# Layer norm by Ln and Exp under one activation table, eight token tiles transposed as pairs of 64 rows, and a new order of blocks 0 to 11 in an attention kernel

## The chip, the cores and the metric

The kernel runs on one core of a Trainium2 chip. The metric is the device time in microseconds of one execution; three runs of the kernel before gave 785.58, 786.32 and 788.21 us, median 786.32.

The core's engines work side by side, each through its own queue in order: TensorE (PE) multiplies matrices, VectorE (DVE), ScalarE (ACT) and GpSimd (POOL) work on elements, and SyncE (SP) issues most of the DMAs. A matmul writes to PSUM, from where DVE or ACT copies its result to SBUF. Engines wait for each other through semaphores only.

## The reference

The core of what is computed, with S = 2048 tokens, D = 640, 32 heads of 192, and a window of 512 keys per head:

```python
xn = _layernorm(x, axis=-1)                       # (x - m) / sqrt(v + 1e-5)
q = (xn @ wq).reshape(B, Sq, Hq, Dh)
k, v = k_cache[:, :, Sk - W:, :], v_cache[:, :, Sk - W:, :]
p = _softmax(einsum("bhqd,bhkd->bhqk", q, k) * (Dh ** -0.5), axis=-1)
s = einsum("bhqk,bhkd->bhqd", p, v).reshape(B, Sq, Hq * Dh) @ wo
...
r = xn @ w_r                                      # the two best tokens by r
idx = argsort(-r)[:, :2]
y = (silu(x_sel @ w_gate) * (x_sel @ w_up)) @ w_down * sigmoid(r_sel)
g = silu(xn + scatter of y to the rows idx)
return x + s * g
```

The output is 1 x 2048 x 640 in bf16. The change lies in the layer norm, in the transposes behind it, and in the order of the first part of the attention.

## The kernel before

Tokens are 16 tiles of 128 rows; four tiles make a token group (t5 = 0 to 3). Heads go in groups of four, two pairs each. A *step* is a head group, a token group and a head pair; it has two *blocks*, and a block covers two tiles (a = 0, 1) of one head pair. There are 128 blocks.

A block b goes through these items:

- **S.b.a** (scores, line 350): six matmuls of 64 rows into one of two PSUM tiles of two banks each (pool ps_s). A third S therefore waits until the exponentials of the one two before it are done.
- **M.b.a** (row_max, line 362): the negated row maximum on DVE.
- **E.b.a** (exps, line 382): two exponentials on ACT, then a DMA transpose of the result on SP's queue (for each a by itself where the item ends in .s or split is set, else one for both after a = 1).
- **P.b** (o_item, line 457): 32 matmuls with v; DVE or ACT scales the output (lines 449 and 452, letters v and a), and a DMA transpose follows. It stands two blocks behind S.
- **W.k** (w_item, line 504): 24 matmuls with wo; the sums go to s_acc.

Ahead of a step stand its queries: **q.i.c** (q_whole, line 294) makes one of three columns with 128-row matmuls; **qa** and **qb** (q_phase, line 315) make one or two columns with 64-row matmuls in two phases, the second of which waits for a later row maximum. All but S share four PSUM banks (pool ps_f) during the first 12 blocks; a new tile waits until the bank that it gets has been read.

**The head.** Blocks 0 to 11 are written out by hand in the list FIRST (line 651), read token by token by first (line 571); every engine gets its instructions in the order of that list. In it also stands all of the layer norm, group by group as x arrives:

- lx, lk, lq, x, k, v, wq, wo (and gk, gq, gv, gw for head group 1) issue loads on SP or ACT; x.2 loads token group 2 into the buffer that group 0 has used.
- bn and st are statistics of half a tile on DVE (bn_stats, with bn_aggr after the second half); **sa.t5.q.c** (rows, line 543) does the same for tile q on ACT, by a sum (c = 0) and a sum of squares (c = 1), with tiny GpSimd steps behind it.
- dev is a square root on ACT for one tile of group 0, app a reciprocal and the normalisation on DVE.
- nw.t5.j is one of seven steps for the deviation of a whole group (rsqrt_parts, line 218: Ln, Exp, an addition on GpSimd, three DVE steps of one Newton round; then nmr = -mean x rstd).
- **ap.n** normalises tile n on GpSimd, ACT or DVE (letters g, a, v), **turn.n** transposes it: five 128 x 128 transposes on PE into one bank, and one copy to xnT.
- ko, kT, kturn, gT: K reordered on GpSimd and transposed; wd copies half of a wo piece to the other 64 partitions on GpSimd (line 150, 1.78 us each), which W reads.
- exp loads the activation table that has both Ln and Exp. Ahead of it, the square root of line 253 uses another table.

From block 12 on a loop (line 1001) goes through BLOCK, the same items in a fixed order:

```python
BLOCK = "A S0 M0 W m E0 B S1 M1 P E1 l".split()
```

The expert's input (m_gather, line 803) has its own layer norm on 2 rows around block 40.

Of the kernel before, what the change touches and what calls it, by code (L numbers as in the profile page):

```python
# [21 lines left out]
def kernel(ctx, tc, A_x, A_k_cache, A_v_cache, A_wq, A_wo, B_x, B_w_r, B_w_gate, B_w_up, B_w_down, out):  # L22
# [158 lines left out]

    def ln_apply(eng, n, src):
        if eng == "a":
            nc.scalar.activation(out=xn[:, n, :], in_=src, func=ACT.Identity, bias=nmr[:, n:n + 1], scale=rstd[:, n:n + 1])
            return
        (nc.gpsimd if eng == "g" else nc.vector).tensor_scalar(
            out=xn[:, n, :], in0=src, scalar1=rstd[:, n:n + 1], scalar2=nmr[:, n:n + 1], op0=ALU.mult, op1=ALU.add)
# [30 lines left out]
    def rsqrt_parts(var_ap, out_ap):  # L218

        T = {}  # L220

        def ln():
            T["v"] = small.tile([P, 4], FP32, name="nw_v")
            T["a"] = small.tile([P, 4], FP32, name="nw_a")
            nc.scalar.activation(out=T["a"], in_=var_ap, func=ACT.Ln, bias=eps_t[:, 0:1], scale=1.0)

        def ex():
            nc.scalar.activation(out=out_ap, in_=T["a"], func=ACT.Exp, scale=-0.5)
# [43 lines left out]
    def turn_tile(n, copy):  # L272
        tp = f_tile([P, DC, P], BF16, "tp")
        for dc in range(DC):
            nc.tensor.transpose(out=tp[:, dc, :], in_=xn[:, n, dc * P:(dc + 1) * P], identity=ident)  # L275
        copy(out=xnT[:, n], in_=tp)  # L276

# [811 lines left out]
```

## Time and profile before

| what | value |
|---|---|
| median of three runs | 786.32 us |
| the profiled execution, whole / span of its trace | 785.81 / 784.0 us |
| PE busy | 771.7 us (98%) |
| DVE, ACT, POOL busy | 561.2, 566.2, 327.1 us |
| granted TensorE clock, mean | 0.999 |
| S.0.0 starts / S.12.0, the first of the loop, starts | 10.53 / 85.39 us |

A profile row by line and tile reads: line, engine, operation, output <- input, shapes, count | busy us, mean ns of one | idle of its engine ahead of it and what ended most of it. A row in order of time reads: start in us, length in us, engine, line, operation, tiles, count, and in brackets the idle time ahead of it with what released it. A row of a stage reads: its bounds and length, then busy time (and instructions) of PE, PE's weight loads, DVE, ACT and POOL, the granted clock, the DMA share and GB/s. In the chain of waits a row is a piece of the chain that ended last: start, length, engine, tile and line.

### The profile page before, as it was taken

Reading aid. Unit: us, or ns where it says so; the run is one execution under the profiler, and the core shown is the slowest. Engines: PE = TensorE matmul, PEld = TensorE weight load, DVE = VectorE, ACT = ScalarE, POOL = GpSimd, SP = SyncE. Lnnn points to the kernel's source line nnn. Section 1 sums busy time; section 2 is a strip of 40 time slices with the busy share of each in tenths; the row PEclk is TensorE's granted clock in tenths of the full one; section 3 lists DMA queues with packets and bytes.
Section 4 is the critical chain, followed back from the end, with each engine's and each line's share of the span. In section 5 each row is a group of like instructions: output and inputs, shape, how many; then the busy total and the mean of one; then the engine's idle time right before and its main releaser. Section 6 shows DMA issues by size and latency. Waiting matters only on the chain.

```text
span 784.0 us, 27247 instructions
## 1 busy us (share of the span) xinstructions
PE 771.7 (98%) x11384; PEld 572.0 (73%) x11384; DVE 561.2 (72%) x952; ACT 566.2 (72%) x1420; POOL 327.1 (42%) x281
## 2 busy tenths in 40 slices
...
GB/s 233 201 173 171 173 177 184 147 193 161 169 213 177 180 200 203 185 178 189 204 187 195 187 188 200 173 189 173 179 172 174 150 189 165 187 181 158 196 197 104
DMA packets 447132, 142.19 MB, mean 181 GB/s; under 512 B 414180, under 2 KB 446438, under 8 KB 447008
## 3 DMA queue, kind: packets, MB, share of 16 engines
...
q0 software_dynamic: 1024, 2.85, 1.3%
...
## 4 chain that ended last, share of the span: by engine, by line
PE 93%; DVE 4%; ACT 2%; DMA 0%; issue 0%; DVEq 0%; ACTq 0%
PE w L482 26%; PE q_ps L332 24%; PE o_ps L435 21%; PE s L359 20%; DVE nm L364 1%; PE q_ps L301 1%; ACT pexp L386 1%; DMA x_in<-in_A_x_dram 0%; DVE stats L538 0%; DVE o_sb L449 0%; ACT xnT L276 0%; DVE qT L305 0%; PE gu_ps L836 0%; PE tp L275 0%; DVE stats L248 0%
## 5 line engine op out<-in xcount | busy, mean ns | idle before, releaser
L364 DVE TENSOR_REDUCE nm<-s 128x2 f32<-128x1024 f32 x256 | 313.0, 1223 | 153.3 <-PE s L359 151.2
L386 ACT ACTIVATE pexp<-s,nm 128x512 bf16<-128x512 f32 x508 | 342.6, 688 | 94.7 <-DVE nm L364 91.0
L332 PE MATMUL q_ps<-xnT,wq_g 64*128 64x512 bf16 (+1 forms) x2340 | 232.7, 323 | 0.0
L482 PE MATMUL w<-wo_g,oT 64*128 64x320 bf16 x3072 | 231.4, 296 | 0.0
L359 PE MATMUL s<-kT,qT 64*128 64x512 bf16 x1536 | 211.6, 376 | 1.7 <-ACT pexp L386 1.4
L482 PEld LDWEIGHTS <-oT 64*128 64x128 bf16 x3072 | 172.0, 94 | 55.7 <-DMA oT<-o_sb 0.5
L435 PEld LDWEIGHTS <-pT 64*128 64x128 bf16 x4096 | 176.3, 94 | 30.6 <-issue 2.8
L435 PE MATMUL o_ps<-v_sb,pT 64*128 64x192 bf16 (+1 forms) x4096 | 193.7, 243 | 2.8 <-DMA pT<-pexp 1.6
L452 ACT ACTIVATE o_sb<-o_ps,rl 128x192 bf16<-128x192 f32 x250 | 91.6, 418 | 97.3 <-PE o_ps L435 88.3
L332 PEld LDWEIGHTS <-wq_g 64*128 64x128 bf16 x2340 | 125.1, 100 | 46.5 <-DVE qT L305 0.5
L150 POOL COPY wo_g<-wo_g 64x1920 bf16<-64x1920 bf16 x32 | 56.9, 1781 | 195.4 <-DMA wo_g<-in_A_wo_dram 180.2
L359 PEld LDWEIGHTS <-qT 64*128 64x128 bf16 x1536 | 84.9, 94 | 56.5 <-issue 2.4
L515 DVE TENSOR_TENSOR s_acc<-s_acc,w 128x320 f32<-128x320 f32 x192 | 84.9, 484 | 30.7 <-PE w L482 30.7
L386 ACT ACTIVATION_READ_ACCUMULATOR pexp<-s,nm 128x1 f32 x460 | 94.0, 204 | 0.0
L344 ACT ACTIVATE qT<-q_ps 128x1024 bf16<-128x1024 f32 x114 | 92.2, 809 | 0.1
L449 DVE TENSOR_TENSOR o_sb<-o_ps,rl 128x384 bf16<-128x384 f32 x131 | 73.0, 557 | 12.1 <-PE o_ps L435 2.2
L926 POOL TENSOR_SCALAR yh<-y_bc,oh 128x640 f32<-128x640 f32 x32 | 60.4, 1886 | 5.7 <-DMA y_bc<-y_d 2.9
L120 POOL COPY k_perm<-k_raw 128x768 bf16<-128x768 bf16 x30 | 24.3, 827 | 89.0 <-DMA k_raw<-in_A_k_cache_dram 64.3
L927 POOL TENSOR_TENSOR xn<-xn,yh 128x640 bf16<-128x640 bf16 x32 | 45.0, 1406 | 2.7
L913 POOL TENSOR_SCALAR tz<-tz 128x640 f32<-128x640 f32 x16 | 11.7, 728 | 63.7 <-ACT tz L912 63.7
L986 POOL TENSOR_TENSOR s_acc<-s_acc,x_fin 128x640 f32<-128x640 f32 x16 | 22.4, 1400 | 11.8 <-DMA x_fin<-in_A_x_dram 10.9
L914 POOL TENSOR_TENSOR xn<-tz,xn 128x640 bf16<-128x640 f32 x16 | 22.4, 1400 | 1.3
...
## 6 DMA issues: line engine op xcount, KB each, us to landing
...
```

What stands on the lines that cost most here:

```text
L150: nc.gpsimd.tensor_copy(out=grp[g][("wo", pr)][half(1), cs, :], in_=grp[g][("wo", pr)][half(0), cs, :])
L332: mm = nc.tensor.matmul(q_ps[k][:, 0:n] if type(q_ps) is list else q_ps[:, k, 0:n], lhsT=wq[half(r), dc, c:2 * Dh:3], rhs=xnT[half(r), tok ...
L344: nc.scalar.activation(out=out, in_=q_ps[:, :, 0:n], func=ACT.Copy, scale=scale)
L359: nc.tensor.matmul(s_of[b, a][:, r, :], lhsT=qT_of[i][half(r), c, u * P:(u + 1) * P], rhs=grp[g][("kT", pr)][half(r), :, c, :], start=(c = ...
L364: rm = nc.vector.tensor_reduce(out=nm_of[b, a], in_=s_of[b, a], axis=AX.X, op=ALU.max, negate=True)
L386: nc.scalar.activation(out=p_of(b, a)[:, :, hh, :].rearrange("p (x j) e -> p x j e", x=2), in_=s_of[b, a][:, hh, :].rearrange("p (j e x) - ...
L435: nc.tensor.matmul(o_of[b][r][:, a, 0:n], lhsT=pT_ring[half(r), b % RP, a, k, :], rhs=v_ring[half(r), (g * PAIRS + pr) % RV, k, 0:n], star ...
L449: nc.vector.tensor_tensor(out=o_sb, in0=src, in1=rl[:, r].unsqueeze(2).unsqueeze(3).to_broadcast([P, 2, 3, HK]), op=ALU.mult)
L452: nc.scalar.activation(out=o_sb[:, a], in_=src[:, a], func=ACT.Copy, scale=rl[:, r, a:a + 1])
L482: nc.tensor.matmul(w_ps[r][:, 0:cs.stop - cs.start], lhsT=oT_ring[half(r), bs[pr] % RT, c, :], rhs=grp[g][("wo", pr)][half(r), c, cs], sta ...
L515: nc.vector.tensor_tensor(out=acc, in0=acc, in1=src, op=ALU.add)
L926: nc.gpsimd.tensor_scalar(out=yh, in0=M["y_bc"][:, j, :], scalar1=M["oh"][:, n, j:j + 1], scalar2=None, op0=ALU.mult)
```

## The change

- **The deviation.** For all groups, rstd is Exp(-0.5 Ln(var + eps)) on ACT (ln_rstd); the Newton round, the addition on GpSimd and group 0's square root and reciprocal are gone. nw has two steps now: ln_rstd, and nmr. The token exp, which loads the table with Ln and Exp, stands ahead of all ACT work; before it stood behind M.0.0.
- **The normalisation.** DVE takes (x - mean) x rstd, GpSimd x rstd + nmr; ACT takes none. The expert's norm takes (x - mean) x rstd too.
- **The pairs.** Tiles 4 to 11 are turned two at a time (token tt, turn_pair): 20 transposes of 64 rows against a 64 x 64 identity, the upper 64 rows of both tiles into one bank and the lower ones into another, and two copies of 640 elements per partition.
- **q_phase** can take two tiles of a step (ha, hb; not used in the new list) and copy its result on either engine. Step 3 has its columns 0 and 1 by qa and qb now.
- **The order.** FIRST is new throughout. Statistics on ACT: tiles 8, 9, 11, 12, 14 (before 12, 13, 14), so ten passes for six. x.2 is read first by sa.2.0.0, which stands behind q.1.2 and ahead of S.1.0. wq.1 is loaded ahead of k.1.0; wd.1 to wd.3 stand in blocks 3 to 5 with sa passes ahead of them on GpSimd's queue. E.4.0, E.8.0 and E.9.0 send their transposes by halves.

```diff
+    def ln_rstd(out, var):
+        t = small.tile([P, 4], FP32, name="ln_v")[:, 0:out.shape[-1]]
+        nc.scalar.activation(out=t, in_=var, func=ACT.Ln, bias=eps_t[:, 0:1], scale=1.0)
+        nc.scalar.activation(out=out, in_=t, func=ACT.Exp, scale=-0.5)
+
+
+    def ln_nmr(bs):
+        nc.vector.scalar_tensor_tensor(out=nmr[:, bs], in0=mv[:, bs, 0], scalar=-1.0, in1=rstd[:, bs], op0=ALU.mult, op1=ALU.mult)
+
     def ln_apply(eng, n, src):
-        if eng == "a":
-            nc.scalar.activation(out=xn[:, n, :], in_=src, func=ACT.Identity, bias=nmr[:, n:n + 1], scale=rstd[:, n:n + 1])
-            return
-        (nc.gpsimd if eng == "g" else nc.vector).tensor_scalar(
-            out=xn[:, n, :], in0=src, scalar1=rstd[:, n:n + 1], scalar2=nmr[:, n:n + 1], op0=ALU.mult, op1=ALU.add)
-
-    def ln_nmr(mean_ap, rstd_ap, nmr_ap):
-        nc.vector.scalar_tensor_tensor(out=nmr_ap, in0=mean_ap, scalar=-1.0, in1=rstd_ap, op0=ALU.mult, op1=ALU.mult)
+        if eng == "g":
+            nc.gpsimd.tensor_scalar(out=xn[:, n, :], in0=src, scalar1=rstd[:, n:n + 1], scalar2=nmr[:, n:n + 1], op0=ALU.mult, op1=ALU.add)
+        else:
+            nc.vector.tensor_scalar(out=xn[:, n, :], in0=src, scalar1=mv[:, n, 0:1], scalar2=rstd[:, n:n + 1], op0=ALU.subtract, op1=ALU.mult)
...
-    def rsqrt_parts(var_ap, out_ap):
-
-        T = {}
-
-        def ln():
-            T["v"] = small.tile([P, 4], FP32, name="nw_v")
-            T["a"] = small.tile([P, 4], FP32, name="nw_a")
-            nc.scalar.activation(out=T["a"], in_=var_ap, func=ACT.Ln, bias=eps_t[:, 0:1], scale=1.0)
-
-        def ex():
-            nc.scalar.activation(out=out_ap, in_=T["a"], func=ACT.Exp, scale=-0.5)
-
-        def v():
-            nc.gpsimd.tensor_scalar(out=T["v"], in0=var_ap, scalar1=EPS, scalar2=None, op0=ALU.add)
-
-        def s1():
-            nc.vector.scalar_tensor_tensor(out=T["a"], in0=out_ap, scalar=-0.5, in1=out_ap, op0=ALU.mult, op1=ALU.mult)
-
-        def s2():
-            nc.vector.tensor_tensor(out=T["a"], in0=T["a"], in1=T["v"], op=ALU.mult)
-
-        def s3():
-            nc.vector.scalar_tensor_tensor(out=out_ap, in0=T["a"], scalar=1.5, in1=out_ap, op0=ALU.add, op1=ALU.mult)
-        return [ln, ex, v, s1, s2, s3]
...
+    def first_apply(n):
+        ln_apply("v", n, x_in[0][:, n, :])
+
     def first_dev(n):
-        nc.scalar.activation(out=rstd[:, n:n + 1], in_=mv[:, n, 1:2], func=ACT.Sqrt, bias=eps_t[:, 0:1], scale=1.0)
-
-    def first_apply(n):
-        nc.vector.reciprocal(out=rstd[:, n:n + 1], in_=rstd[:, n:n + 1])
-        nc.vector.tensor_scalar(out=xn[:, n, :], in0=x_in[0][:, n, :], scalar1=mv[:, n, 0:1], scalar2=rstd[:, n:n + 1],
-                                op0=ALU.subtract, op1=ALU.mult)
+        ln_rstd(rstd[:, n:n + 1], mv[:, n, 1:2])
...
+    def turn_pair(n, es):
+        tp = [f_tile([P, 2, DC, P // 2], BF16, "tp") for _ in range(2)]
+        for u in range(2):
+            for dc in range(DC):
+                for r in range(2):
+                    nc.tensor.transpose(out=tp[r][:, u, dc, :], in_=xn[half(r), n + u, dc * P:(dc + 1) * P], identity=ident[half(r), half(r)])
+        for r in range(2):
+            copies[es[r]](out=xnT[:, n:n + 2, :, half(r)], in_=tp[r])
...
-        return ([bn(q, c) for q in range(4) for c in range(nsub)], rsqrt_parts(mv[:, bs, 1], rstd[:, bs]) + [lambda: ln_nmr(mv[:, bs, 0], rstd[:, bs], nmr[:, bs])],
+        return ([bn(q, c) for q in range(4) for c in range(nsub)], [lambda: ln_rstd(rstd[:, bs], mv[:, bs, 1]), lambda: ln_nmr(bs)],
...
+        elif op == "tt":
+            turn_pair(n[0], e)
...
-    lx.0.s lx.1.a lk.0.s lk.1.s lq.0.a lx.2.s lx.3.s v.0 x.1.0 bn.0.0 bn.1.0 x.1.1 bn.1.1 dev.1 bn.0.1 app.1 dev.0 k.1.0 app.0 bn.2.0 turn.0.a bn.3.0 bn.3.1 turn.1.a v.1 kturn.av bn.2.1 wq.1 dev.3 q.0.2.0.a k.1.1 q.0.0.0.v dev.2 v.2 q.0.1.0.a
-    ko.1 app.2 app.3 st.1.0
-    S.0.0 M.0.0 exp x.2 turn.2.a turn.3.a S.0.1 kT.1 M.0.1 st.1.1 E.0.0.s st.1.2 wo.0 q.0.1.1.a q.0.0.1.a q.0.2.1.v E.0.1
-    S.1.0 wo.1 st.1.3 st.1.4 S.1.1 M.1.0 st.1.5 E.1.0.s q.1.1.a M.1.1 q.1.2.a E.1.1 st.1.6 q.1.0.v st.1.7 nw.1.0
-    S.2.0 nw.1.1 nw.1.2 M.2.0 wo.2 S.2.1 nw.1.3 nw.1.4 nw.1.5 M.2.1 nw.1.6 st.2.0 E.2.0.s ap.7.g ap.6.v P.0.vv E.2.1
-    S.3.0 M.3.0 ap.4.a v.3 S.3.1 turn.6.a ap.5.g wd.0 turn.5.a turn.4.v turn.7.v E.3.0.s st.2.1 st.2.2 P.1.va M.3.1 wo.3 st.2.3 E.3.1 q.2.1.a q.2.2.v st.2.4 wd.1 q.2.0.v P.2.va
-    S.4.0 M.4.0 S.4.1 E.4.0 x.3 M.4.1 st.2.5 q.3.1.a E.4.1 wd.2 st.2.6 st.2.7 nw.2.0 q.3.2.a nw.2.1 nw.2.2
-    S.5.0 M.5.0 nw.2.3 E.5.0 nw.2.4 q.3.0.v S.5.1 wd.3 nw.2.5 sa.3.0.0 nw.2.6 M.5.1 E.5.1 sa.3.2.0 W.0.v ap.10.g
-    S.6.0 ap.11.g M.6.0 gk.0 E.6.0 ap.9.g ap.8.v W.1.v P.3.av S.6.1 M.6.1 P.4.va
-    S.7.0 st.3.6 E.6.1 turn.10.v turn.11.v turn.9.a turn.8.v sa.3.0.1 M.7.0 S.7.1 E.7.0 gk.1 q.4.2.v gq.0 q.4.1.v q.4.0.a
-    qa.5.0.1 sa.3.1.0
-    S.8.0 M.7.1 go.0 E.7.1 st.3.7 gw.0 sa.3.2.1 sa.3.1.1 nw.3.0 nw.3.1 M.8.0 W.2.v qb.5.0.1 nw.3.2 nw.3.3 nw.3.4 nw.3.5 P.5.av S.8.1 M.8.1 gq.1 nw.3.6 E.8.0 E.8.1 P.6.va ap.15.v
-    qa.5.2 ap.12.v
-    S.9.0 S.9.1 M.9.0 ap.14.g turn.12.v turn.14.v E.9.0 ap.13.g qb.5.2 turn.13.v M.9.1 turn.15.v
-    S.10.0 gT.0 E.9.1 gk.2 gk.3 P.7.vv W.3.v M.10.0 E.10.0 S.10.1 gv.0 P.8.vv W.4.a
-    qa.6.0.1 M.10.1 gd.0
-    S.11.0 E.10.1 M.11.0 B.11 go.1 E.11.0 W.5.v qb.6.0.1 P.9.av q.6.2.v S.11.1 M.11.1 E.11.1 gw.1 gv.1
+    lx.0.s lx.1.a lk.0.s lk.1.s lq.0.a exp lx.2.s lx.3.s v.0 x.1.0 bn.1.0 x.1.1 bn.0.0 bn.0.1 wq.1 dev.0 bn.1.1 dev.1 k.1.0 app.1 app.0 bn.2.0 bn.2.1 k.1.1 bn.3.0 turn.1.a turn.0.a v.1 bn.3.1 dev.2 app.2 kturn.av q.0.2.0.a v.2 q.0.0.0.v dev.3 app.3 q.0.1.0.a turn.2.a
+    S.0.0 st.1.0 turn.3.a M.0.0 st.1.1 st.1.2 x.2 ko.1 S.0.1 st.1.3 kT.1 E.0.0.s q.0.2.1.a q.0.0.1.a M.0.1 q.0.1.1.a E.0.1 wo.0 st.1.4 q.1.2.a sa.2.0.0
+    S.1.0 st.1.5 st.1.6 q.1.1.a S.1.1 M.1.0 M.1.1 E.1.0.s q.1.0.v st.1.7 E.1.1 v.3 nw.1.0
+    S.2.0 M.2.0 S.2.1 ap.4.v nw.1.1 M.2.1 ap.7.g E.2.0.s ap.6.v E.2.1 P.0.av sa.2.0.1 wd.0 wo.1 tt.6.vv wo.2
+    S.3.0 ap.5.v S.3.1 sa.2.1.0 tt.4.va M.3.0 P.1.av M.3.1 q.2.2.v E.3.0.s st.2.4 E.3.1 sa.2.3.0 q.2.1.v sa.2.1.1 wo.3 q.2.0.v P.2.av
+    S.4.0 wd.1 qa.3.0.1 M.4.0 S.4.1 E.4.0.s M.4.1 x.3 q.3.2.a st.2.5 S.5.0 wd.2 E.4.1 qb.3.0.1.aa M.5.0 E.5.0 P.3.av wd.3 sa.2.3.1
+    S.5.1 M.5.1 W.0.v nw.2.0 S.6.0 nw.2.1 E.5.1 gk.0 ap.8.g gq.0 ap.11.g M.6.0 st.3.6 sa.3.0.0 W.1.v
+    S.6.1 M.6.1 E.6.0 P.4.va ap.9.g S.7.0 ap.10.g E.6.1 st.3.2 tt.10.vv tt.8.va M.7.0 S.7.1 q.4.0.a E.7.0 st.3.3 M.7.1 gk.1 sa.3.2.0 q.4.1.v q.4.2.v E.7.1 qa.5.0.1
+    S.8.0 sa.3.0.1 sa.3.2.1 gq.1 st.3.7 M.8.0 W.2.a nw.3.0 nw.3.1 qb.5.0.1 P.5.va ap.14.g
+    S.8.1 E.8.0.s M.8.1 E.8.1 P.6.va ap.12.v ap.15.v gw.0 go.0 qa.5.2 S.9.0 M.9.0 ap.13.g
+    S.9.1 E.9.0.s turn.14.v turn.12.v qb.5.2 M.9.1 gk.2 turn.15.v turn.13.a S.10.0 E.9.1 M.10.0 W.3.a gT.0 gk.3 P.7.va P.8.va E.10.0 W.4.v
+    S.10.1 qa.6.0.1 M.10.1 S.11.0 M.11.0 E.10.1 go.1 W.5.a B.11 qb.6.0.1 P.9.vv q.6.2.a
+    S.11.1 M.11.1 E.11.0 E.11.1 gv.0 gd.0 gv.1 gw.1
...
-            M["rs2"] = M["s"].tile([2, 2], FP32, name="rs2")
+            M["rs2"] = M["s"].tile([2, 1], FP32, name="rs2")
...
-            ln_nmr(mv2[:, 0:1], rs2[:, 0:1], rs2[:, 1:2])
-            nc.vector.tensor_scalar(out=M["xsel"][0:2, :], in0=M["xg"], scalar1=rs2[:, 0:1], scalar2=rs2[:, 1:2], op0=ALU.mult, op1=ALU.add)
+            nc.vector.tensor_scalar(out=M["xsel"][0:2, :], in0=M["xg"], scalar1=mv2[:, 0:1], scalar2=rs2, op0=ALU.subtract, op1=ALU.mult)
```

More of the change, by code (lines that the diff above doesn't have):

```diff
@@ L311, with q_scale, q_phase @@
     q_of = {}
-    count = {"S": 0}
-    last_max = {}
-    def q_phase(i, cs, ph):
+    count = {"n": 0}
+    seen = {}
+    def q_scale(e, out, in_):
+        if e == "v":
+            nc.vector.tensor_scalar(out=out, in0=in_, scalar1=scale, scalar2=None, op0=ALU.mult)
+        else:
+            nc.scalar.activation(out=out, in_=in_, func=ACT.Copy, scale=scale)
+    def q_phase(i, cs, ph, hf=None, es="aa"):
         g, t5, pr = steps[i]
```

32 lines of the change are left out of this document (19 added, 13 removed).

## The prediction

> **What bounds the kernel now.** I read the page first, then busy time by stage, then the chain of waits, then the instructions in order of time for the first 88 us, which is all that the new order touches.
>
> ```profile
> span 784.0 us, 27247 instructions
> PE 771.7 (98%) x11384; PEld 572.0 (73%) x11384; DVE 561.2 (72%) x952; ACT 566.2 (72%) x1420; POOL 327.1 (42%) x281
> ```
> ```profile
> 0.00:20.00 20.00, 16.30 (x112) 8.64 (x113) 15.95 (x41) 12.42 (x23) 2.29 (x8) 1.00 0.95 232
> 20.00:37.00 17.00, 13.38 (x165) 8.33 (x164) 13.94 (x34) 10.35 (x20) 7.28 (x6) 1.00 1.17 205
> 37.00:85.00 48.00, 47.38 (x604) 30.80 (x602) 40.24 (x80) 33.51 (x70) 15.98 (x31) 1.00 0.93 172
> 85.00:760.00 675.00, 674.98 (x10144) 508.59 (x10142) 475.64 (x769) 499.05 (x1281) 282.68 (x218) 1.00 1.09 182
> ```
>
> In each row the second figure after the stage is PE's busy time; the third last figure is the granted clock, 1.00 throughout. From 85 us on PE idles 0.02 us in 675. So the time changes only by how much sooner PE reaches the loop behind block 11, and by PE work removed. Before 85 us PE idles 3.70 + 3.62 + 0.62 = 7.9 us. That, and PE work saved, is all there is to win.
>
> The milestones that I carry through (S is a block's score matmuls, line 359):
>
> ```profile
> 21.47 1.47 PE L359 MATMUL s<-kT,qT 64*128 64x512 bf16 x12 [0.79 <-ACT pexp L386]
> 22.41 1.23 DVE L364 TENSOR_REDUCE nm<-s 128x2 f32<-128x1024 f32 x1 [0.35 <-ACT nw_a L225]
> 36.40 1.53 PE L359 MATMUL s<-kT,qT 64*128 64x512 bf16 x12
> 52.91 0.82 PE L359 MATMUL s<-kT,qT 64*128 64x512 bf16 x6 [0.44 <-ACT pexp L386]
> 58.11 0.81 PE L359 MATMUL s<-kT,qT 64*128 64x512 bf16 x6
> 85.39 0.81 PE L359 MATMUL s<-kT,qT 64*128 64x512 bf16 x6
> ```
>
> They are S.2.0, its maximum, S.4.0, S.7.1, S.8.0 and S.12.0, the first of the loop.
>
> **Prices.** On the chain of waits, where PE is the link, a piece lasts what it really takes from PE:
>
> ```profile
> 53.73 3.35 PE q_ps L301 x15
> ...
> 60.55 1.08 PE q_ps L332 x10
> ...
> 68.49 0.66 PE tp L275 x10
> 69.15 0.75 PE s L359 x6
> 69.91 1.33 PE o_ps L435 x32
> 71.24 1.63 PE w L482 x24
> 72.87 0.65 PE s L359 x6
> ```
>
> So S 0.65, P 1.33, W 1.63, a whole q column 1.12, a q phase 1.08, two turned tiles 0.66. S behind a transpose is 0.75: a change between 128-row and 64-row matmuls costs 0.10.
>
> ```profile
> L386 ACT ACTIVATE pexp<-s,nm 128x512 bf16<-128x512 f32 x46 | 29.1, 688 | 12.4 <-DVE nm L364 9.1 <-PE o_ps L435 3.2
> L364 DVE TENSOR_REDUCE nm<-s 128x2 f32<-128x1024 f32 x24 | 29.0, 1212 | 2.0 <-PE s L359 0.9 <-ACT pexp L386 0.5 <-ACT nw_a L225 0.4
> L538 DVE BATCH_NORM_STATS2 stats<-x_in 128x6 f32<-128x320 bf16 x18 | 8.4, 473 | 0.0
> L305 DVE TENSOR_SCALAR qT<-q_ps 128x512 bf16<-128x512 f32 x7 | 4.8, 680 | 2.0 <-PE q_ps L301 2.0
> L276 DVE COPY xnT<-tp 128x640 bf16<-128x640 bf16 x9 | 4.0, 480 | 0.4 <-PE tp L275 0.4
> L553 ACT ACTIVATE xn<-x_in,sums 128x640 bf16<-128x640 bf16 x3 | 2.5, 841 | 0.0
> L549 ACT ACTIVATE xn<-x_in 128x640 bf16<-128x640 bf16 x3 | 2.2, 733 | 0.5 <-DMA x_in<-in_A_x_dram 0.5
> L225 ACT ACTIVATE nw_a<-mv,eps_t 128x4 f32<-128x4 f32 x3 | 0.9, 306 | 1.0 <-DVE mv L540 0.6 <-POOL mv L554 0.3
> L228 ACT ACTIVATE rstd<-nw_a 128x4 f32<-128x4 f32 x3 | 0.6, 212 | 0.1
> ```
> ```profile
> 13.46 1.28 ACT L386 ACTIVATE pexp<-s,nm 128x512 bf16<-128x512 f32 x2
> 14.62 0.69 ACT L307 ACTIVATE qT<-q_ps 128x256 bf16<-128x256 f32 x2
> ...
> 49.16 0.56 DVE L449 TENSOR_TENSOR o_sb<-o_ps,rl 128x384 bf16<-128x384 f32 x1
> 49.64 1.21 DVE L364 TENSOR_REDUCE nm<-s 128x2 f32<-128x1024 f32 x1
> ```
>
> An engine takes its next instruction a little before the listed end: the exponentials last 1.28 but release ACT after 14.62 - 13.46 = 1.16, o_sb lasts 0.56 but releases DVE after 0.48. I therefore walk with the listed duration less 0.08 (DVE) or 0.12 (ACT) for the next in the queue, and the full one for whoever reads the result. The forecast leans on this choice; the other end is a rival below.
>
> **Edit 1, the deviation.** Tiles 0 to 3 change a square root and a DVE reciprocal for Ln 0.31 + Exp 0.21; groups 1 to 3 lose three tiny DVE steps and a GpSimd one each, and DVE's own applies no longer wait for nmr. Tiles 0 and 1 come out within 0.1 us of before: one x tile's copy ends 0.3 later, but turn.1 goes first now. The second table load goes:
>
> ```profile
> 11.00 1.28 ACT L593 ACT_TABLE_LOAD   x1
> ```
>
> After it ACT's two tile copies lead to E.0.0 at 13.46; without it E.0.0 starts when its maximum is ready, at 13.05. So 0.4 is won of the 1.28, and it ends in the next wait.
>
> **Edit 2, the pairs.** The trace has such transposes in the tail:
>
> ```profile
> 767.73 0.65 PE L412 MATMUL tp_p<-ident,wq_g 64*128 64x64 bf16 x32
> 768.20 1.50 PE L435 MATMUL o_ps<-v_sb,pT 64*128 64x192 bf16 x32
> ```
>
> 32 in 0.47, so a pair's 20 in 0.30 instead of 0.66: four pairs save 1.44 of PE work. The copies stay 640 elements each (0.48 on DVE).
>
> **Edit 3, the order.** Four statistics passes go from DVE (0.47 each) to ACT. One of them, sa.2.0.0, now stands in ACT's queue before q.1.1's copy, E.1.0 and E.1.1, and reads the x load of group 2, which before was read first by DVE's st.2.0, a block later:
>
> ```profile
> 11.61 0.37 SPq L97 DMA_DIRECT2D x_in<-in_A_x_dram  x1
> ...
> x_in<-in_A_x_dram SPq DMA_DIRECT2D x1, 640.0 KB, 7.6
> ...
> GB/s 0 0 102 305 318 360 297 271 347 277 202 210 360 364 248 161 256 339 330 189 166 312 327 36 63 212 208 219 182 68 298 147 304 217 199 289 27 312 211 199
> ```
>
> It lands at 11.61 + 7.6 = 19.2. The load is the last of those that the head issues, and the rate (slices of 0.75 us) falls only behind 17.25: the engines drain this same list of bytes in either order, so issuing x.2 some 0.5 earlier doesn't land it earlier. I take 19.2; bounds 17.3 (the fall of the rate) and 21 (the K transpose, now issued near 16.5, gets ahead of its last bytes).
>
> *The walk.* (a) E.0.1 ends at 17.1 and ACT is free at 17.4 after q.1.2's copy; it stands until 19.2. Then sa.2.0.0 0.75 and q.1.1's copy 0.48 (20.43), E.1.0 ends at 21.71, E.1.1 at 22.87. S.2.0 needs E.1.0's scores bank: 21.75, 0.3 **later** than before.
>
> (b) From M.2.0 (22.68) DVE is back to back: 4 maxima x 1.14, 3 applies x 0.35, nmr 0.08, two P outputs x 0.75 (o_sb and the small reciprocals ahead of it), 3 pair copies x 0.40, a statistics step 0.40, 3 q copies x 0.60 = 10.6, and 0.6 waiting for P.0 and pair 4; the last q copy is done at 33.95. Before, the same stretch held four statistics steps more (st.2.0 to st.2.4, now st.2.4 alone) and the Newton steps. P.0 finds its transposed exponentials at about 23.8: the load of wq.1 now goes ahead of both K pieces and v.1 behind them, so K's copies and its transpose on SP's queue, behind which block 0's two transposes stand, start some 0.7 sooner. PE runs P.2 from 32.96 to 34.29, so S.4.0 starts at 34.3 instead of 36.4: **-2.1**.
>
> (c) Behind S.4.0 PE has 7 S 4.55, q of step 3 3.28, two P 2.66, two W 3.26, pairs 0.60, q of step 4 3.35, the first phase of step 5 1.08 = 18.8, and S.4.0 itself 0.65, with three stalls: 0.14 at S.6.1, 0.46 for GpSimd's xn of tile 10, 0.88 at S.7.1. The last two come from ACT, which between 39 and 50 runs five exponentials, two statistics passes, Ln and Exp back to back. S.8.0 would come at 55.3; four changes of row mode on PE's own path add 0.4: 55.7 against 58.11, **-2.4**. Cover: W.0 (41.5) needs the three wo doublings that now stand in GpSimd's queue behind sa.2.1.1; they end near 41.2; a later end would delay W.0 one for one from 42.7, where its last quarter reads them.
>
> (d) S.8.0 to S.12.0 has the same work in both (27.28 before); my walk gives 27.1, so -0.2. Blocks 4, 8 and 9 send their transposes in halves now, two places on SP's queue for one; the products that read them come two blocks later, 5 us and more behind the issue, and hide it. The expert's normalisation near block 40 loses one DVE step on 2 rows, where the row from 85 on has no PE idle: nothing.
>
> The sum is **-2.6**. Against the profiled execution's own 785.81 that is 783.2; that execution lies 0.5 under the median of 786.32, and I give the median's: **783.7**.
>
> *The shared port.* One row bears on DVE and GpSimd normalising side by side:
>
> ```profile
> 25.69 0.83 DVE L186 TENSOR_SCALAR xn<-x_in,rstd,nmr 128x640 bf16<-128x640 bf16 x1
> ...
> 47.76 0.43 DVE L186 TENSOR_SCALAR xn<-x_in,rstd,nmr 128x640 bf16<-128x640 bf16 x1
> ```
>
> The first ran beside GpSimd's, the second alone. In the walk GpSimd's tile 7 ends 0.1 before DVE's tile 6, so I add nothing; overlap costs 0.40 in (b). The Trainium skill (SBUF — State Buffer, "Who interferes with whom") says that a DVE instruction in a two-port mode and a GpSimd instruction exclude each other for a whole instruction, the later one blocked; by that rule the sum would be -2.2 if tile 7 slips by 0.1, and the 0.83 agrees with it.
>
> **The rivals.**
> 1. *The load is there.* If x.2 lands by 17.4, E.1.0 starts at 18.7 and S.2.0 only waits for q.1.0's copy (20.25); P.0's late input then takes up part: 1.2 to 1.6 more, -4, **782.3**. For it: the rate falls at 17.25. Against: 7.6 to landing.
> 2. *ACT is the bound.* With full listed durations for the queue too, (c)'s ACT chain (five exponentials x 0.12, as much again in copies and passes) and the DVE chain of (b) stretch; the same walk has S.4.0 at 35.1, S.7.1 at 52.0, S.8.0 at 57.2 and loses more at S.10.0: -0.5, **785.8**. For it: ACT takes the four passes (3.2 us) just where it stalls S.7.1. Against: the 1.16 above.
> 3. *Slower: the wait at the head of ACT's queue.* Each us that x.2 lands behind 19.2 comes through one for one: no gain from 21.8 on, slower by more than 0.3% from 24.2; at 25 it is +3.2, **789.5**. For it: the load is last in a queue that K's transpose now shares earlier, and E.1.0, E.1.1 and the Ln stand behind it. Against: that takes over 13 us from issue where 7.6 were measured.
>
> **How the numbers follow.** A measurement of this kernel tells 0.3% (2.4 us) from no change. The forecast has 0.48, and its own range (782.3 to 785) lies on both sides of 783.96: 0.30 faster, 0.18 the same. Rival 1 has 0.22 (faster), rival 2 0.16 (same), rival 3 0.14 (slower; a late load is the least known price here). So faster 0.52, same 0.34, slower 0.14. The range: down to rival 1 with (c)'s 1.5 us of stalls gone too, 780.6; up past rival 2 into rival 3, 788.2.
>
> **What would show it.** Right: one table load; ACT idle from about 17.4 until sa.2.0.0 at 19.2, released by the x load; S.2.0 near 21.8, S.4.0 near 34.3, S.7.1 released by an exponential, S.8.0 near 55.7, S.12.0 near 82.8; 20 pair transposes in 0.30; PE still without idle time behind. Wrong: S.2.0 near 20.3 (rival 1), S.7.1 behind 51.5 (rival 2), S.2.0 behind 24 (rival 3), or a later loop that does not keep the shift.

## The result, and the profile after

The kernel after took 784.11 us (median of 15 runs, 783.19 to 785.37) against 786.20 for the kernel before in the same sitting: ratio 0.9969, interval 0.9960 to 0.9978. That is 2.1 us less by the medians; 783.7 was forecast. The profiled execution is the run of 783.19, the fastest of the 15.

The page of after, span and busy time (PE, its weight loads, DVE, ACT, POOL), and then its stages, in the columns shown ahead of the prediction:

```profile
span 781.3 us, 27352 instructions
PE 770.6 (99%) x11434; PEld 577.6 (74%) x11434; DVE 553.4 (71%) x925; ACT 570.1 (73%) x1440; POOL 327.6 (42%) x284
```
```profile
0.00:20.00 20.00, 17.82 (x114) 8.96 (x114) 15.22 (x37) 12.09 (x28) 2.62 (x10) 1.00 1.05 245
20.00:37.00 17.00, 14.48 (x201) 8.90 (x202) 14.35 (x29) 14.40 (x32) 6.59 (x11) 1.00 1.16 198
37.00:85.00 48.00, 46.91 (x653) 30.13 (x652) 34.56 (x66) 36.46 (x79) 16.43 (x29) 1.00 0.97 173
85.00:760.00 675.00, 674.71 (x10152) 516.25 (x10150) 476.52 (x772) 498.18 (x1284) 285.54 (x221) 1.00 1.08 182
```

PE idles 5.8 us ahead of 85 us where it idled 7.9, and 0.29 instead of 0.02 between 85 and 760. ACT's share of the stage from 20 to 37 went from 10.35 to 14.40 us and is now level with DVE's.

The milestones of after in order of time (start, length, and in brackets the idle time ahead with its releaser): ACT's first statistics pass, S.2.0, S.4.0, S.7.1, S.8.0, S.12.0. The row ahead of them is the x load that the pass reads, at its issue; the last one says how long such a load took from issue to landing.

```profile
11.27 0.39 SPq L97 DMA_DIRECT2D x_in<-in_A_x_dram  x1
18.73 0.74 ACT L549 ACTIVATE xn<-x_in 128x640 bf16<-128x640 bf16 x1 [1.07 <-DMA x_in<-in_A_x_dram]
21.25 0.82 PE L359 MATMUL s<-kT,qT 64*128 64x512 bf16 x6 [1.43 <-ACT pexp L386]
33.71 0.81 PE L359 MATMUL s<-kT,qT 64*128 64x512 bf16 x6
49.69 0.82 PE L359 MATMUL s<-kT,qT 64*128 64x512 bf16 x6 [0.69 <-ACT pexp L386]
54.89 0.81 PE L359 MATMUL s<-kT,qT 64*128 64x512 bf16 x6
82.03 0.82 PE L359 MATMUL s<-kT,qT 64*128 64x512 bf16 x6
...
x_in<-in_A_x_dram SPq DMA_DIRECT2D x1, 640.0 KB, 7.4
```

So the gain is made in one stretch: S.2.0 comes 0.2 sooner than before, S.4.0 2.7, S.8.0 3.2, S.12.0 3.4. Behind that, part is given back: from S.12.0 to the end of the span before took 698.6 us and after 699.3, and 2.7 are left. In the other twelve profiled executions below this last part took 699.0 to 700.9, so the profiled before lay at its short end. A start ahead of 85 us is read to about 0.3 us in a trace: S.0.0, up to which eight of these kernels are alike, starts between 10.75 and 11.31. The length of a stretch is steadier: S.8.0 to S.12.0 took 27.14 or 27.15 in all eleven traces of the new order.

### The profile page after: what moved, and what is told of

It reads as the page before. It is cut to its first block, busy times and chain, and to the rows that moved or that the text cites. A ratio compares the mean times of both kernels' runs of the same rounds, so it can differ in the third digit from the quotient of the medians.

```text
span 781.3 us, 27352 instructions
## 1 busy us (share of the span) xinstructions
PE 770.6 (99%) x11434; PEld 577.6 (74%) x11434; DVE 553.4 (71%) x925; ACT 570.1 (73%) x1440; POOL 327.6 (42%) x284
## 3 DMA queue, kind: packets, MB, share of 16 engines
q8 instruction: 89, 1.46, 0.8%
## 4 chain that ended last, share of the span: by engine, by line
PE 94%; ACT 3%; DVE 2%; DMA 1%; issue 0%; ACTq 0%; POOL 0%; DVEq 0%; POOLq 0%
PE w L482 26%; PE q_ps L331 25%; PE o_ps L435 21%; PE s L359 20%; DMA x_in<-in_A_x_dram 1%; PE q_ps L290 1%; ACT pexp L386 1%; DVE nm L364 1%; ACT o_sb L452 0%; PE gu_ps L835 0%; PE tp L254 0%; DVE stats L229 0%; ACT xn L553 0%; ACT xn L549 0%; ACT xnT L255 0%
## 5 line engine op out<-in xcount | busy, mean ns | idle before, releaser
L331 PE MATMUL q_ps<-xnT,wq_g 64*128 64x512 bf16 (+1 forms) x2360 | 235.7, 323 | 0.3 <-DVE th L838 0.2
L482 PEld LDWEIGHTS <-oT 64*128 64x128 bf16 x3072 | 175.8, 94 | 52.0
L331 PEld LDWEIGHTS <-wq_g 64*128 64x128 bf16 x2360 | 127.2, 99 | 47.4 <-issue 1.0
L309 ACT ACTIVATE qT<-q_ps 128x1024 bf16<-128x1024 f32 (+2 forms) x122 | 96.1, 791 | 0.4 <-PE q_ps L331 0.3
```

The source lines that it names most:

```text
L309: nc.scalar.activation(out=out, in_=in_, func=ACT.Copy, scale=scale)
L331: mm = nc.tensor.matmul(q_ps[k][:, 0:n] if type(q_ps) is list else q_ps[:, k, 0:n], lhsT=wq[half(r), dc, c:2 * Dh:3], rhs=xnT[half(r), tok ...
L482: nc.tensor.matmul(w_ps[r][:, 0:cs.stop - cs.start], lhsT=oT_ring[half(r), bs[pr] % RT, c, :], rhs=grp[g][("wo", pr)][half(r), c, cs], sta ...
```

## The experiments

Most are the kernel after with one edit; x2_later_sa23 has two and order_alone three, and dev_alone and pairs_alone are the kernel before with one. Starts are those of one profiled execution each; ratios are to the kernel before, run beside them, over five rounds.

| run | S.2.0 | S.4.0 | S.8.0 | S.12.0 | ratio, interval |
|---|---|---|---|---|---|
| before | 21.47 | 36.40 | 58.11 | 85.39 | 1 |
| after | 21.25 | 33.71 | 54.89 | 82.03 | 0.9969, 0.9960–0.9978 |
| x2_later | 20.65 | 33.16 | 54.33 | 81.48 | 0.9956, 0.9943–0.9968 |
| x2_halves | 20.91 | 33.38 | 54.81 | 81.95 | 0.9963, 0.9950–0.9975 |
| x2_behind_kT | 24.30 | 37.96 | 59.14 | 86.28 | 1.0016, 1.0006–1.0027 |
| x2_later_sa23 | 20.81 | 33.33 | 55.28 | 82.43 | 0.9975, 0.9967–0.9984 |
| two_tables | 21.58 | 34.05 | 55.23 | 82.38 | 0.9967, 0.9955–0.9980 |
| newton_back | 21.34 | 34.47 | 56.23 | 83.38 | 0.9967, 0.9954–0.9979 |
| pairs_undone | 21.01 | 34.00 | 55.18 | 82.32 | 0.9981, 0.9970–0.9992 |
| stats_on_dve | 21.07 | 34.16 | 55.24 | 82.39 | 0.9971, 0.9962–0.9980 |
| loads_before | 21.29 | 33.76 | 55.45 | 82.60 | 0.9970, 0.9958–0.9982 |
| dev_alone | 21.27 | 35.46 | 56.58 | 83.87 | 0.9997, 0.9985–1.0008 |
| pairs_alone | 21.58 | 37.27 | 58.90 | 86.19 | 0.9995, 0.9985–1.0006 |
| order_alone | 21.41 | 35.08 | 56.84 | 83.99 | 0.9995, 0.9984–1.0006 |

### The wait for the x load

**x2_later** puts the first pass behind E.1.1.

```diff
-    ... q.1.2.a sa.2.0.0
-    S.1.0 ... E.1.1 v.3 nw.1.0
+    ... q.1.2.a
+    S.1.0 ... E.1.1 v.3 nw.1.0 sa.2.0.0
```

> The sum of squares' first pass on group 2 (sa.2.0.0) stands behind E.1.1 and the first Ln and Exp instead of ahead of q.1.1's copy; nothing else is moved. Theory (the x load at the head of ACT's queue sets S.2.0): ACT no longer idles 1.07 us at 17.7, S.2.0 starts at about 20.3 instead of 21.25, set by q.1.0's copy on DVE, and the rest follows by 0.5 to 1.0: S.4.0 near 33.0, about 783.3 us. Rival (DVE's chain sets it, the load is only the last of several): S.2.0 may move, S.4.0 stays within 0.3 of 33.7, 784.1 us.

S.2.0 in x2_later, in order of time:

```profile
20.65 1.47 PE L359 MATMUL s<-kT,qT 64*128 64x512 bf16 x12 [0.79 <-DVE qT L294]
```

The wait for an exponential is gone and one for DVE's copy of q.1.0 stands in its place: 0.6 is won of the 1.07 that ACT stood, and 0.55 of it reaches S.12.0. By the times this version isn't told apart from after (the intervals overlap); its ratio is the lowest of the series.

**x2_halves** issues the same load as two.

```diff
-    ... st.1.2 x.2 ko.1
+    ... st.1.2 x.2.0 x.2.1 ko.1
```

> The x load of group 2 is issued as two loads of two tiles, in the same place. Theory (ACT waits for the landing and nothing else): the first half lands about 1.1 us before the whole (327 KB fewer at some 300 GB/s), ACT starts sa.2.0.0 near 17.7 instead of 18.73, S.2.0 at about 20.3, S.4.0 near 33.0, about 783.3 us. Rival 1 (landing is bounded by the drained queue, both halves land together): no change, 784.1. Rival 2 (DVE's chain): S.2.0 moves, S.4.0 does not.

ACT's pass starts at 17.84 without a wait, though everything ahead of it began 0.3 later in this run than in after. The first tile was there before ACT was free, so in after ACT stood for the rest of a load of which the pass reads only the first tile. S.2.0 and S.4.0 come 0.33 sooner than in after; 0.25 of it is lost again by S.8.0.

**x2_behind_kT** issues the load behind K's transpose.

```diff
-    ... st.1.2 x.2 ko.1 S.0.1 st.1.3 kT.1 E.0.0.s
+    ... st.1.2 ko.1 S.0.1 st.1.3 kT.1 x.2 E.0.0.s
```

> The x load of group 2 is issued behind K's transpose on SP's queue, at about 16 instead of 11.3 us. Theory (its landing sets S.2.0 one for one, which was the mechanism of the slower rival): it lands 2 to 3 us later than 18.7, S.2.0 and S.4.0 are later by as much, about 786.3 us. Rival (later stalls take it up): S.2.0 later, but S.8.0 within 1 us, below 785.1.

ACT and then PE of x2_behind_kT in order of time, and its stages around S.2.0 (the granted clock is third from the end):

```profile
21.79 0.74 ACT L549 ACTIVATE xn<-x_in 128x640 bf16<-128x640 bf16 x1 [4.13 <-DMA x_in<-in_A_x_dram]
...
24.30 2.75 PE L359 MATMUL s<-kT,qT 64*128 64x512 bf16 x12 [4.48 <-ACT pexp L386]
```
```profile
22.00:23.00 1.00, 0.00 (x0) 0.00 (x0) 0.00 (x0) 1.00 (x4) 0.29 (x2) 1.00 1.29 269
23.00:24.00 1.00, 0.00 (x0) 0.00 (x0) 0.00 (x0) 1.00 (x3) 0.12 (x1) 0.64 0.79 175
24.00:25.00 1.00, 0.69 (x4) 0.30 (x5) 0.00 (x0) 1.00 (x3) 0.00 (x0) 0.50 0.25 82
25.00:30.00 5.00, 5.00 (x64) 3.93 (x62) 3.46 (x8) 3.37 (x8) 0.87 (x1) 0.50 0.83 161
30.00:31.00 1.00, 1.00 (x17) 0.55 (x13) 1.00 (x3) 1.00 (x3) 0.00 (x0) 0.94 1.07 183
```

The load is read 3.06 later than in after and S.2.0 comes 3.05 later: rival 3's mechanism, one for one. But S.4.0 and all that follows come 4.25 later. PE stood for 4.48 us, its clock was halved for some 6.8 us (0.64 in the slice from 23 and 0.94 in that from 30 put the ends at 23.3 and 30.1), and twelve S matmuls took 2.75 where they take 1.46. The whole gain of the change is lost; by the ratio the kernel is 1.3 us slower than before, with an interval of 0.5 to 2.1.

**x2_later_sa23** adds to x2_later a move of the second pass of tile 11 ahead of E.5.0, for S.7.1's wait.

```diff
-    ... qb.3.0.1.aa M.5.0 E.5.0 P.3.av wd.3 sa.2.3.1
+    ... qb.3.0.1.aa M.5.0 sa.2.3.1 E.5.0 P.3.av wd.3
```

> The statistics pass of group 2's first tile stands behind E.1.1, as in the run that did this alone, and sa.2.3.1 now stands ahead of E.5.0 too. Theory: S.7.1's wait (0.69 in the kernel after) hangs on ACT's chain sa.2.3.1, Ln, Exp, nmr, M.6.0, E.6.1, of which sa.2.3.1 stands behind two exponentials that nobody needs so soon; ahead of them it ends about 1.2 sooner, so S.7.1 starts at 48.5 to 48.8 (49.13 with the first move alone), S.8.0 at 53.8 to 54.1 (54.33), S.12.0 at 81.0 to 81.3 (81.48), and the ratio to before is 0.995 or a little under. Rival: the exponentials of block 5 that are put off delay S.6.1 and P.5 by as much, and S.12.0 stays at 81.4 to 81.8 with a ratio of 0.9955 to 0.996.

GpSimd and PE of x2_later_sa23 in order of time:

```profile
40.98 0.21 POOL L554 TENSOR_SCALAR mv<-sums 128x1 f32<-128x1 f32 x1 [3.21 <-ACT xn L553]
41.24 1.78 POOL L150 COPY wo_g<-wo_g 64x1920 bf16<-64x1920 bf16 x1
...
43.08 0.56 PE L482 MATMUL w<-wo_g,oT 64*128 64x320 bf16 x5 [0.85 <-POOL wo_g L150]
...
50.08 0.82 PE L359 MATMUL s<-kT,qT 64*128 64x512 bf16 x6 [0.69 <-ACT pexp L386]
```

Neither theory foresaw this. The pass has a tiny step on GpSimd, which now stands ahead of the last wo doubling; the doubling ends at 43.0 instead of 40.2 in x2_later, and W.0 waits 0.85 for it. That is the cover that the prediction named (W.0 reads the doublings, one for one from 42.7 on). S.7.1's wait stayed at 0.69, but with W.0 in the way this run alone doesn't tell what it hangs on; stats_on_dve below tells more.

### The deviation

**two_tables** brings back the square root, the reciprocal and the second table load.

```diff
-        ln_rstd(rstd[:, n:n + 1], mv[:, n, 1:2])
+        nc.scalar.activation(out=rstd[:, n:n + 1], in_=mv[:, n, 1:2], func=ACT.Sqrt, bias=eps_t[:, 0:1], scale=1.0)
...
-    lx.0.s ... lq.0.a exp lx.2.s ... turn.2.a
+    lx.0.s ... lq.0.a lx.2.s ... exp turn.2.a
```

> Tiles 0 to 3 by square root and reciprocal as before, and the second table load back behind q.0.1's copy; all else as changed. Theory (the wait for the x load absorbs it): the load of 1.28 us delays E.0.0 by 0.3 to 0.8, but ACT's idle 1.07 us ahead of sa.2.0.0 shrinks by as much and S.2.0 stays within 0.3 of 21.25: 784.1 us. Rival (the table load is on the path): S.2.0 and all behind it later by up to 1.28, 785.4 us.

S.1.0 came 0.76 later, but ACT still waited 0.89 for the x load, which was read at 19.06, 0.33 later than in after; S.2.0 lost 0.33 too, S.12.0 0.35. So the table load went into the wait for x, as the prediction had it; that the 0.33 is the load's own is likely, not shown.

**newton_back** puts a Newton round between Exp and nmr of groups 1 to 3: one addition on GpSimd and three tiny DVE steps each. It also puts group 1's nmr (nw.1.1) ahead of tile 4's normalisation.

```diff
+        nc.gpsimd.tensor_scalar(out=v, in0=mv[:, bs, 1], scalar1=EPS, scalar2=None, op0=ALU.add)
+        nc.vector.scalar_tensor_tensor(out=h, in0=rstd[:, bs], scalar=-0.5, in1=rstd[:, bs], op0=ALU.mult, op1=ALU.mult)
+        nc.vector.tensor_tensor(out=h, in0=h, in1=v, op=ALU.mult)
+        nc.vector.scalar_tensor_tensor(out=rstd[:, bs], in0=h, scalar=1.5, in1=rstd[:, bs], op0=ALU.add, op1=ALU.mult)
...
-    ... S.2.1 ap.4.v nw.1.1 M.2.1 ...
+    ... S.2.1 nw.1.1 ap.4.v M.2.1 ...
```

> The Newton round is back behind Ln and Exp for groups 1 to 3 (one GpSimd and three dependent DVE steps each, ahead of nmr; group 1's nmr now ahead of tile 4's normalisation). Theory: three steps of about 0.2 each stand on the DVE chain ahead of M.2.1 and again ahead of M.6.0: S.4.0 0.5 to 0.8 later, S.8.0 0.7 to 1.4 later, about 785.1 us. Rival (tiny steps, hidden): 784.1 us.

DVE of newton_back in order of time, between the maximum of S.2.0 and the first normalisation:

```profile
23.41 0.15 DVE L193 SCALAR_TENSOR_TENSOR nw_a<-rstd 128x4 f32<-128x4 f32 x1
23.67 0.16 DVE L194 TENSOR_TENSOR nw_a<-nw_a,nw_v 128x4 f32<-128x4 f32 x1
23.87 0.16 DVE L195 SCALAR_TENSOR_TENSOR rstd<-nw_a,rstd 128x4 f32<-128x4 f32 x1
24.06 0.16 DVE L199 SCALAR_TENSOR_TENSOR nmr<-mv,rstd 128x4 f32<-128x4 f32 x1
24.14 0.44 DVE L205 TENSOR_SCALAR xn<-x_in,mv,rstd 128x640 bf16<-128x640 bf16 x1
```

Steps of 0.16 that wait for each other start 0.19 to 0.26 apart, 0.65 in all from the first to nmr, and S.2.0 to S.4.0 is 0.67 longer than in after. Group 2's round costs 0.58 more between S.4.0 and S.8.0. At S.12.0 the round costs 1.35, at the ends of these two executions 2.9; the ratio doesn't show it.

**dev_alone** is the kernel before with this edit alone (Ln and Exp for all tiles, one table, no Newton round).

```diff
-    ... lq.0.a lx.2.s ... S.0.0 M.0.0 exp x.2 ...
+    ... lq.0.a exp lx.2.s ... S.0.0 M.0.0 x.2 ...
...
-        return [ln, ex, v, s1, s2, s3]
+        return [ln, ex]
```

> The kernel before with the first edit alone: one activation table, Ln and Exp for all 16 tiles, no Newton round, no reciprocal, (x - mean) x rstd on DVE; order, pairs and loads as before. Theory (the edits are small, the order carries the gain): E.0.0 starts 0.4 sooner (13.05 for 13.46), S.2.0 0.3 to 0.4 sooner, and between S.2.0 and S.4.0 DVE loses 0.5 of Newton steps; S.4.0 at 35.5 to 35.8 (36.40 before), S.12.0 at 84.3 to 84.7 (85.39), ratio 0.9985 to 0.9993. Rival (the deviation carries half of the gain, as putting the Newton round back in the new order cost 1.35 and the second table 0.33 at S.12.0): S.12.0 at 83.6 to 84.0, ratio near 0.998.

At S.12.0 it is the rival's number, 83.87: 1.5 of the 3.4. By the times nothing of it is left. The trace shows where one execution lost half of it again, in the loop:

```profile
114.75 1.53 PE L485 MATMUL w<-wo_g,oT 64*128 64x320 bf16 x20 [0.67 <-DVE o_sb L452]
```

Neither before nor after has that wait, and no more than the one trace shows it.

### The pairs

**pairs_undone** turns tiles 4 to 11 one by one at the places of the pairs.

```diff
-    ... tt.6.vv ... tt.4.va ... tt.10.vv tt.8.va ...
+    ... turn.6.v turn.7.v ... turn.4.v turn.5.a ... turn.10.v turn.11.v turn.8.v turn.9.a ...
```

> Tiles 4 to 11 turned one by one with 128-row transposes again, in the places of the pairs. By the prediction's term: 8 x 0.33 instead of 4 x 0.30 of PE work, 1.44 us more; where PE waits anyway (around pair 4 and ahead of S.7.1) part of it is hidden. Theory: S.12.0 0.7 to 1.4 later than 82.14, about 785.0 us. Rival (all of it fills PE's idle time): S.12.0 within 0.3, 784.1 us.

From S.2.0 to S.4.0 it takes 12.99 against 12.46: 0.53 for the first two pairs. From S.4.0 to S.8.0 both take 21.18: the other two pairs' time goes into S.7.1's wait, which is 0.25 here and 0.69 in after. (The expectation's 82.14 is after's 82.03.) Its x load was read 0.24 sooner than after's, so that S.12.0 shows only 0.29 of it. The pairs are worth 0.5 and not 1.44.

**pairs_alone** is the kernel before with the pairs at the places of the single turns.

```diff
-    ... turn.6.a ap.5.g wd.0 turn.5.a turn.4.v turn.7.v ...
+    ... tt.6.av ap.5.g wd.0 tt.4.av ...
-    ... turn.10.v turn.11.v turn.9.a turn.8.v ...
+    ... tt.10.vv tt.8.av ...
```

> The kernel before with the pairs alone: tiles 4 to 11 turned two at a time at the places of the single turns. Theory (what PE saves, two pairs' 0.72 ahead of S.4.0 and 0.72 behind it, is taken up by DVE's chain, which sets the end there, but for 0.2 to 0.5): S.4.0 at 36.0 to 36.4 (36.40 before), S.12.0 at 84.9 to 85.3 (85.39), ratio 0.9993 to 1. Rival (the prediction's term: PE's work goes straight into the time): 1.44 less, S.12.0 at 83.95, ratio 0.998.

In this trace neither theory's time came: S.4.0 was 0.9 later than in before. The stages of pairs_alone from 28 to 33 us and PE's P.1 among them:

```profile
28.00:29.00 1.00, 0.46 (x19) 0.35 (x20) 1.00 (x1) 1.00 (x2) 1.00 (x1) 1.00 1.21 163
29.00:30.00 1.00, 0.45 (x7) 0.45 (x8) 1.00 (x4) 1.00 (x3) 1.00 (x2) 0.77 1.07 208
30.00:31.00 1.00, 1.00 (x18) 1.00 (x15) 0.86 (x3) 0.40 (x1) 1.00 (x2) 0.50 0.69 134
31.00:32.00 1.00, 1.00 (x17) 0.94 (x12) 0.00 (x0) 0.00 (x0) 1.00 (x1) 0.50 2.33 54
32.00:33.00 1.00, 1.00 (x6) 0.29 (x3) 0.61 (x3) 0.44 (x2) 0.67 (x1) 0.53 0.16 27
```
```profile
29.55 2.77 PE L444 MATMUL o_ps<-v_sb,pT 64*128 64x193 bf16 x32 [1.06 <-DVE xnT L285]
```

PE was done with the pairs sooner and stood longer for DVE's copies, and its clock was halved for 3.4 us: P.1 took 2.77 for 1.50, and a step's q columns 3.74 for 3.42 (before's). These two make 1.6, so at full clock S.4.0 would not have come later than in before (an estimate). Not every execution seems to have this: the mean granted clock is 0.997 in four of the twelve, the profiled one among them, and 0.999 or 1.000 in the others. So this trace doesn't decide between the theories. The medians of the two kinds are 786.7 and 786.6; by the times the pairs alone change nothing that can be measured.

### The order

**stats_on_dve** gives the passes of tiles 9 and 11 back to DVE.

```diff
-    ... sa.2.1.0 ... sa.2.3.0 q.2.1.v sa.2.1.1 ... sa.2.3.1
+    ... st.2.2 ... st.2.6 q.2.1.v st.2.3 ... st.2.7
```

> The statistics of tiles 9 and 11 on DVE again (four half tiles, in the places of the four ACT passes); tile 8 stays on ACT. Theory (DVE is the chain from S.2.0 to S.4.0, ACT the one to S.7.1): three of the four, 0.41 each and an aggregate, fall ahead of S.4.0: 0.8 to 1.4 later there; S.7.1's wait for its exponential (0.69) shrinks, so S.12.0 is 0.3 to 1.0 later than 82.03: about 784.7 us. Rival 1 (ACT is the bound all along): faster, 783.3. Rival 2 (PE alone): 784.1.

From S.2.0 to S.4.0 it takes 0.63 more; S.4.0 waits 0.64 for DVE's q copy. So DVE has no room for these steps. It isn't DVE that ends the stretch in after, though: there PE starts the first pair at 25.37, when DVE's normalisation is done, and is busy for 8.21 of the 8.34 us from then to S.4.0. The last wait in it is one for ACT, as the chain of waits of after shows (start, length, what):

```profile
25.00 1.26 ACT pexp L386 x2
...
28.41 0.59 ACT xnT L265
...
29.04 3.40 PE q_ps L290 x15
32.44 1.44 PE o_ps L435 x32
```

S.7.1's wait was expected to shrink, as ACT has four passes less, one of them in the last 10 us ahead of S.7.1. It is 0.69 as in after:

```profile
50.04 0.82 PE L359 MATMUL s<-kT,qT 64*128 64x512 bf16 x6 [0.69 <-ACT pexp L386]
```

The chain to it runs through DVE here, whose reciprocal ACT awaits for 1.13 us ahead of its half of P.4's output. So S.7.1 doesn't hang on ACT's pass alone.

**loads_before** issues SP's first loads in before's order, wq.1 behind v.1.

```diff
-    ... bn.0.1 wq.1 dev.0 ... bn.2.1 k.1.1 bn.3.0 turn.1.a turn.0.a v.1 bn.3.1 dev.2 ...
+    ... bn.0.1 dev.0 ... bn.2.1 bn.3.0 turn.1.a turn.0.a v.1 wq.1 bn.3.1 k.1.1 dev.2 ...
```

> The loads in SP's queue in the order of the kernel before: k.1.0, v.1, wq.1, k.1.1, v.2 instead of wq.1, k.1.0, k.1.1, v.1, v.2. Theory (the new load order lets K's transpose and block 0's two transposes go 2 to 3 us sooner, so that P.0 no longer waits): K's transpose starts at about 17 instead of 14.5, P.0 waits 0.5 to 1 us for its second half again, S.4.0 0.5 to 1.0 later than 33.7, about 784.8 us. Rival (the x load of group 2 and DVE hide it): S.4.0 within 0.3, 784.1 us.

K's transpose was issued at 16.93 instead of 14.51 and q.1.2 waited 0.8 for wq.1, but S.4.0 lost only 0.05; 0.5 appeared between S.4.0 and S.8.0. P.0 had its input in time in both. Where the 0.5 comes from stays open.

**order_alone** is the kernel after without the other edits: square root, reciprocal and second table, Newton rounds, single turns (the diffs of two_tables, newton_back and pairs_undone together).

> The kernel after with all three edits taken out and only the new order left: square root, reciprocal and second table for group 0, a Newton round for groups 1 to 3, single turns at the places of the pairs. Theory (what the undone edits cost one by one adds up: 1.35 for Newton, 0.33 for the table, 0.3 for the pairs at S.12.0): S.4.0 at 35.0 to 35.4 (33.71 after, 36.40 before), S.12.0 at 83.8 to 84.2 (82.03 after, 85.39 before), ratio 0.9985 to 0.999: order and edits share the gain about half and half. Rival (the order is the whole gain, and the edits only matter once it is there): S.12.0 at 82.5 to 83, ratio 0.997. Second rival (the order needs the edits): S.12.0 at 85.4 or later, ratio 1 or more.

S.4.0 at 35.08 and S.12.0 at 83.99 are the first theory's numbers: the order alone brings 1.4 at S.12.0. With what the edits cost when undone one at a time (1.35, 0.35, 0.29) that makes 3.39, and 3.36 was measured, so in the traces the parts add up, as far as starts that scatter by 0.3 can say. In the times they don't: each alone measures 0.2 to 0.4 us with an interval of 0.9 either way, and together 2.4 by the ratio. The traces have the loop giving back part in single executions (0.67 and 0.2 in dev_alone); why a small shift should be given back more fully than a large one stays open.

One part of the order stands in no theory: v.3, the last load that P.2 reads. In before it is issued at 30.72 behind transposes on SP's queue and takes 4.4 us to land; P.2's second matmul, the first to read it, starts at 35.13. In dev_alone the load is issued 0.96 sooner and S.4.0 comes 0.94 sooner. The load's issue in before, and P.2 in dev_alone:

```profile
30.72 0.58 SPq L135 DMA_DIRECT2D v_sb<-in_A_v_cache_dram  x1
...
34.19 1.50 PE L438 MATMUL o_ps<-v_sb,pT 64*128 64x193 bf16 x31 [0.47 <-DMA v_sb<-in_A_v_cache_dram]
```

So dev_alone's gain up to S.4.0 comes through this load. In after it is issued at 23.87, and P.2 runs without a wait. No run moves it alone, so its share of the order's 1.4 isn't shown.

## Why the prediction was right

The forecast held in its time and in its place: nearly all of the gain is made between S.2.0 and S.4.0, and behind the head PE is the bound. Some of its reasons didn't hold, and part of the agreement in time is luck. By its steps:

- **Edit 1, the table.** One load, at 1.67 us. E.0.0 started at 13.19 (13.05 said), and the gain ended in the next wait, ACT's for x. Right; two_tables bears it out.
- **(a) x.2 first read by ACT.** ACT was free at 17.66 and waited 1.07 until 18.73 (17.4 and 19.2 said), S.2.0 at 21.25 (21.75). The mechanism was right; the load was 0.5 less late.
- **(b) DVE back to back.** M.2.0 to the last q copy took 11.1 us (11.3 said), S.2.0 to S.4.0 12.46 (12.55). The time is right, the reason in part: DVE holds PE up to 25.37, and from there on PE has 0.13 us without work. P.0 started at 23.05 without a wait (its input was said for 23.8). K's transpose was issued at 14.51, not 16.5, and loads_before shows that this is hidden. GpSimd's tile 7 ended at 24.87 and DVE's tile 6 took 0.44 from 24.88, so they didn't overlap, as the walk has it. The load of v.3 isn't in the walk. What the prediction didn't price by itself is the Newton round: it named the steps among others in the -2.1, and they are 0.67 here and 1.35 in all.
- **(c) to S.8.0.** 21.18 for 21.4. S.7.1 stood 0.69 (0.88 said) and tile 10 0.22 (0.46). Both are shorter than said, and ACT isn't back to back. The chain of waits of after, from ACT's pass to S.7.1 (start, length, what), goes through ACT's pass, Ln and Exp, then through GpSimd and DVE, and ends with P.4's output and an exponential on ACT:

```profile
42.18 0.81 ACT xn L553 x2
...
43.14 0.22 POOL mv L554
...
43.38 0.31 ACT ln_v L185
...
43.71 0.21 ACT rstd L186
...
44.02 0.16 DVE nmr L190
44.18 1.13 DVE nm L364
...
47.75 0.73 ACT o_sb L452 x2
48.48 1.16 ACT pexp L386 x2
```

  ACT stands 0.81 for DVE at the last but one of these, and stats_on_dve, which has taken tile 11's second pass off ACT, keeps the 0.69. The row of after:

```profile
47.75 0.73 ACT L452 ACTIVATE o_sb<-o_ps,rl 128x192 bf16<-128x192 f32 x2 [0.81 <-DVE rl L445]
```

- **(d) to S.12.0.** 27.14 for 27.1.
- **Edit 2, the pairs.** The price of one is right, the place is not:

```profile
25.37 0.47 PE L263 MATMUL tp<-ident,xn 64*128 64x64 bf16 x20 [0.81 <-DVE xn L196]
25.67 1.46 PE L359 MATMUL s<-kT,qT 64*128 64x512 bf16 x12
```

20 transposes from 25.37 to 25.67 are the 0.30 forecast. But the 1.44 of saved PE work is not all on the path: 0.53 of it is, in (b), where the prediction had DVE as the bound, and in (c) S.7.1's wait takes the rest.
- **The sum.** -2.6 was forecast, and -3.36 measured at S.12.0; 0.5 of the difference is the x load. At the end of the spans -2.7 is left, because 0.66 more went between S.12.0 and the end, which the prediction had at nothing. So two errors of nearly one size cancel in the profiled pair: that part is luck. PE was to have no idle time behind the head; from 88 to 760 us it has waits of 0.2 to 0.9 in eleven of the fourteen traces, after's among them (0.2), and none in before's. By the medians the gain is 2.1. Part of what is missing there goes with the clock: six of the 15 executions of after have a granted clock of 0.997 or 0.998 and a median of 784.55, the nine others 0.999 or 1.000 and 783.60. The prediction had no term for that. Its line between faster and the same, 0.3%, lies inside the measured interval (0.22% to 0.40%), so on which side of it the change falls isn't decided. By its own terms the range's lower end is 780.8, not 780.6.
- **Rivals.** Rival 1 (the load is there) was run as x2_later and x2_halves: S.2.0 did wait for the q copy, and in x2_later that is worth 0.55, not the 1.2 to 1.6 given it. Rival 2 (ACT the bound) fell in its time: S.7.1 came at 49.69, where 52.0 was said. With three passes fewer on ACT ahead of it (stats_on_dve), S.4.0 came 0.45 later and not sooner, but in after ACT has next to no room between 25.00 and 29.00 either. Rival 3 was run as x2_behind_kT and is dearer than priced.
